# Program order of an expert chain: the usual side last, a hint for its first branch, narrower turns

## The chip, the cores and the metric

The kernel runs on one core of one Trainium2 chip. The metric is the device time of one execution in microseconds (us); less is better. Engines are called as the profile calls them: PE (TensorE), DVE (VectorE), ACT (ScalarE), POOL (GpSimd), SP (SyncE, which issues most transfers). Each engine has a sequencer that reads its own stream of instructions, and that stream is fetched from memory while the program runs. The trace shows what a sequencer itself does (branches, register loads, semaphores) under PEldq, DVEq, ACTq, POOLq and SPq.

## What is computed

Three layers follow each other, all in float32:

```
x   = attention(q, k, v)             # chunks of 64 tokens, 8 heads, 2 x 576 = 1152 tokens of 512
x   = moe(x, w_gate, w1, w2, cap)    # 8 experts, top 1, at most 288 tokens each
out = sum over e of p[:, e] * (relu(x @ w1[e]) @ w2[e])      # 4 domain experts, dense
```

In the middle layer the expert of a token is the argmax of its gate logits, the tokens of an expert are taken in order until its capacity of 288 is full, the others give zero rows, and a kept row is `gate * (relu(x @ w1[e]) @ w2[e])` with w1 of 512 x 1024 and w2 of 1024 x 512. How many tokens an expert gets is known only on the chip.

## The kernel before, in words

**Products.** Every float32 factor is split into a high part (rounded, dtype fp32r, by ScalarE, `part_hi`, line 114) and a low rest (by VectorE, `part_lo`, line 118), and a product is the sum of high x high, high x low and low x high.

**Attention** (lines 325 to 391) goes over nine blocks of 128 tokens. It also makes the gate logits, the rank of every token in its expert, and one-hot sums `t_ps` that give the tokens of each expert. Expert 0 of the program's order is the one that token 0 chose (`oh0`), so its weights are loaded early. Lines 394 to 445 then count: `cnt` is the tokens of an expert (`n_ps`, cut at the capacity), `large` says whether `cnt` is over `limit` (232 for the first expert, 192 for the others), `form` is 0 for an expert without tokens, 1 for a small and 2 for a large one, and the others are put in the order large, small, empty. PE meanwhile runs 27 products on zeros (`warm`, line 140). `form`, the sum of all tokens (`kept`) and the places of the experts' columns (`o_r`) become registers in lines 768 to 770 (`numbers`, line 545): each engine loads them itself.

**The experts** (lines 520 to 784). `wide(k, W, slots)` computes one expert on W columns with three products per weight tile; `joined(k, W, slots)` does it for at most 192 tokens with two, of 384 and 192 columns, since the high and the low part of x stand side by side. After each eighth or fourth of the work both call `place(i)`, which issues what `chores` (line 667) has put into slot i: the weights of the next expert (load, high, low), and the turn of the next expert's tokens. A turn (`xturn`, line 536) transposes the gathered rows in three pieces of 128, 128 and 32 tokens, for four column blocks; `xsplit` (line 541) makes high and low out of 288 columns. `gather` (line 400) fetches the rows by three indirect transfers.

**The order of the code around the change.** The program holds every sequence of forms as nested branches. `expert_0` stands twice (lines 780 to 783): in the first place for a first expert of at most 232 tokens (chain "a"), in the second for a larger one (chain "b"). Each calls `large_from(1, left, tag)`, which nests "large_k" branches while experts can still be large (`left`, here 5 and 4), and at every depth an Else with `small_from`, which nests "more_k" branches of joined experts. Where no expert with tokens is left, `first_dense` (line 716) computes the first dense layer-1 products, 48 of 384 columns, on the banks. All these ends go through a jump to the code behind the chain, then through line 780's to `late` (line 653: the high and low parts of the second dense weights) and `pick_last` (line 925), which chooses the dense program by `kept`. A branch is written so that its "then" side follows in memory and its Else is jumped to. `hint` (line 664) puts an instruction on PE, early in an expert, that tells its sequencer by a register which side of the next branch is to come: 1 the following code, 0 the Else.

**The dense layers** (line 796 on) are 4 domains x 2 halves x 3 groups of up to 384 tokens: layer 1 is line 824, layer 2 lines 853 and 872. Their first bank is one that first_dense used, so the first product waits until VectorE's line 726 has read it.

With the inputs timed here the first expert has 210 tokens, one other is large (384, cut to 288), four are small and two are empty. So the path is: chain "a", `wide(0, 232)`, "large_1" taken, `wide(1, 288)`, the Else of "large_2", four `joined`, the Else of "more_6", `first_dense`, and out.

Of the kernel before, what the change touches and what calls it, by code (L numbers as in the profile page):

```python
# [9 lines left out]
F32 = mybir.dt.float32  # L10
F32R = mybir.dt.float32r
F16 = mybir.dt.float16
I32 = mybir.dt.int32
ACTF = mybir.ActivationFunctionType
ALU = mybir.AluOpType
AX = mybir.AxisListType
PSUM = bass.MemoryType.PSUM
DRAM = bass.MemoryType.DRAM
ENG = mybir.EngineType

P = 128
NTOK = 1152
# [5 lines left out]
KD = DM // P  # L28
NE = 8
# [7 lines left out]
EPS = 1e-9  # L37
MC = 6
NP = NE + 1
WARM = (8, 4, 2, 27, 4, 3, 4)  # L40

C_ID = 0
C_IO = 128
# [27 lines left out]
def kernel(ctx: ExitStack, tc: tile.TileContext, kqv_d, wg, w_all, dp, cst, out, cap):  # L71
    nc = tc.nc

    XW, W0, CW = 288, 232, 192
    wins = ((0, P), (P, P), (2 * P, XW - 2 * P))
    assert cap <= XW

    ctx.enter_context(tc.manual_schedule(engines={ENG.PE, ENG.Activation, ENG.DVE, ENG.SP}))
# [4 lines left out]
    cp = ctx.enter_context(tc.tile_pool(name="cp", bufs=1))  # L83
    wp = ctx.enter_context(tc.tile_pool(name="wp", bufs=1))
    xrp = ctx.enter_context(tc.tile_pool(name="xrp", bufs=1))
    sp = ctx.enter_context(tc.tile_pool(name="small", bufs=3))

    xt0 = xrp.tile([P, 2 * KD * XW], F32R, name="xt0")
    xrs = [xrp.tile([P, 3, DM], F32, name=f"xr{j}") for j in range(2)]
    cc = cp.tile([P, C_KEEP], F32, name="cc")  # L90
    ident = cc[:, C_ID:C_ID + P]
# [8 lines left out]
    oh0 = cp.tile([P, NE], F32, name="oh0")  # L100
# [4 lines left out]
    wz = cp.tile([P, 512], F16, name="wz")  # L105
# [14 lines left out]
    def bc(ap, n, pos):  # L120
        return ap.unsqueeze(pos).broadcast_to(list(ap.shape[:pos]) + [n] + list(ap.shape[pos:]))


    with ExitStack() as ast:
        ap_ = ast.enter_context(tc.tile_pool(name="attn", bufs=2))
# [10 lines left out]
        def warm(n, tag="s"):  # L136
            if n:
                w_ps = ps.tile([P, 512], F32, tag=tag, bufs=2 if tag == "s" else 1, name="w_ps")
                for i in range(n):
                    nc.tensor.matmul(w_ps, wz[:, 0:P], wz, start=True, stop=True)  # L140
# [184 lines left out]
        for j in range(NT):  # L325
            if 1 <= j < 3:
                warm(WARM[1], "xt")
            a, b, c, d = j, j - 1, j - 2, j - 3
# [41 lines left out]
        n = NT - 1  # L370
# [26 lines left out]
        with nc.allow_low_precision(reason="whole numbers below 2048"):  # L397
            nc.vector.tensor_reduce(out=gidx0, in_=g0, axis=AX.X, op=ALU.add)

        def gather(k, ws=(0, 1, 2)):  # L400
            for w in ws:
                n = wins[w][1]
                ix = gidx[0:n, k, w:w + 1] if k else gidx0[0:n, w:w + 1]
                nc.gpsimd.indirect_dma_start(out=xrs[k % 2][0:n, w, :], out_offset=None, in_=x_d[:, :],  # L404
                                             in_offset=bass.IndirectOffsetOnAxis(ap=ix, axis=0))
# [10 lines left out]
        some, cnt, place, off, form = (st[:, i] for i in range(5))  # L416
        rol2 = sp.tile([P, NE], F32, bufs=1, name="rol2")
        large = sp.tile([P, NE], F32, bufs=1, name="large")
        pr = sp.tile([P, 2, NE, NE], F32, bufs=1, name="pr")
        sel = sp.tile([P, NE, NE], F32, bufs=1, name="sel")  # L420
        pv = sp.tile([P, 3, NE, NE], F32, bufs=1, name="pv")
# [4 lines left out]
        nc.vector.tensor_scalar(out=some, in0=n_ps[:, 0], scalar1=0.0, scalar2=None, op0=ALU.is_gt)  # L426

        nc.vector.tensor_tensor(out=large, in0=cnt, in1=limit, op=ALU.is_gt)
        nc.vector.scalar_tensor_tensor(out=rol2, in0=large, scalar=-8.0, in1=rol, op0=ALU.mult, op1=ALU.add)
        nc.vector.tensor_tensor(out=mrol, in0=bc(rol2, NE, 1), in1=bc(rol2, NE, 2), op=ALU.is_lt)  # L430
        nc.vector.tensor_tensor(out=pr, in0=bc(mrol, 2, 1), in1=bc(st[:, 0:2], NE, 2), op=ALU.mult)
# [88 lines left out]
    with ExitStack() as est:  # L520
# [12 lines left out]
            nc.scalar.copy(hi, src)  # L533
            nc.vector.tensor_tensor(out=lo, in0=src, in1=hi.bitcast(F32), op=ALU.subtract)

        def xturn(k, kd, t, ws):
            for w in ws:
                lo, n = wins[w]
                nc.tensor.transpose(t[:, lo:lo + n], xrs[k % 2][0:n, w, kd * P:kd * P + P], ident[0:n, 0:n])  # L539

        def xsplit(k, kd, t, a=0, b=XW):
            hi_lo(xts[k % 2][:, kd, 0, a:b], xts[k % 2][:, kd, 1, a:b], t[:, a:b])

        def numbers(src, **kw):
            return nc.values_load_multi_w_load_instructions(
                src, min_val=0, skip_runtime_bounds_check_because="whole numbers counted on the chip, within it for any routing", **kw)[1]

        regs = []

# [114 lines left out]
        def hint(label, off):  # L664
            tc.mark_branch_hint_location(label, hint=off, engines=(ENG.PE,))

        def chores(k, small, ahead):

            slots = {}

            def at(i, f, *args):
                slots.setdefault(i, []).append(lambda: f(*args))

            def turn(kd):
                xturn(k + 1, kd, tps[kd % 2], range(3))

            def split(kd):
                xsplit(k + 1, kd, tps[kd % 2])

            def known():  # L680
                regs[:] = numbers(pli[0:1, :], engines=(ENG.SP,), max_val=NE + NDOM - 1)

            if k + 1 < NE:
                for kd in range(KD):
                    at((7, 9, 11, 13)[kd], turn, kd)
                    at((8, 10, 12, 14)[kd], split, kd)
            if k == 0:
                at(0, part_lo, 2, 0)
                at(0, places)
                at(0, known)  # L690
                for h in range(2):
                    at(0, load, 1, 0, h)
                at(1, part_lo, 2, 1)
                for h in range(2):
                    at(1, load, 1, 2, h)
                for n, (j, h) in enumerate(((1, 0), (1, 1), (3, 0), (3, 1))):
                    at(n + 3, part_lo, j, h)
                    at(n + 3, load, 1, j, h)
            else:
                for n, (j, h) in enumerate(((1, 0), (1, 1), (3, 0), (3, 1))):  # L700
                    at((0, 2, 5, 7)[n], part_hi, j, h)
                    i = (1, 3, 6, 8)[n]
                    at(i, part_lo, j, h)
                    at(i, load, k + 1, j, h)
            for n, (j, h) in enumerate(((0, 0), (0, 1), (2, 0), (2, 1))):
                at((8, 9, 11, 13)[n], part_hi, j, h)
                i = (9, 10, 12, 14)[n]
                at(i, part_lo, j, h)
                at(i, load, k + 2, j, h)
            at(3, ahead)  # L710
            if k == 0:
                for n, f in enumerate(dense_rows()):
                    at(7 + n // 2, f)
            return slots

        def first_dense():

            for ff in range(NF):
                o = banks[ff][:, 0:GW]
                c = 0  # L720
                for kd in range(KD):
                    for a, b in ((0, 0), (0, 1), (1, 0)):
                        nc.tensor.matmul(o, w1(0, a, kd)[:, ff * P:ff * P + P], x2[:, b, kd, 0:GW], start=c == 0, stop=c == 3 * KD - 1)  # L723
                        c += 1
                nc.scalar.activation(out=h_first[:, ff, 0], in_=o, func=ACTF.Relu)
                nc.vector.scalar_tensor_tensor(out=h_first[:, ff, 1], in0=o, scalar=0.0, in1=h_first[:, ff, 0].bitcast(F32),
                                               op0=ALU.max, op1=ALU.subtract)

        def ahead(k):
            if 1 < k + 1 < NE:  # L730
                gather(k + 1)

        def small_from(k, tag):
            if k == NE:
                first_dense()
                return
            with tc.If(form_r[k] > 0, label=f"more{tag}_{k}") as more:
                ahead(k + 1)
                joined(k, CW, chores(k, True, lambda: hint(f"more{tag}_{k + 1}", form_r[k] + form_r[k + 1] - 1) if k + 1 < NE else None))
                small_from(k + 1, tag)  # L740
            with more.Else():
                first_dense()

        def large_from(k, left, tag):
            if k == NE or not left:
                small_from(k, f"{tag}_{k}")
                return
            with tc.If(form_r[k] > 1, label=f"large{tag}_{k}") as large:
                ahead(k + 1)
                wide(k, XW, chores(k, False, lambda: hint(f"large{tag}_{k + 1}", form_r[k + 1] // 2) if k + 1 < NE and left > 1 else None))  # L750
                large_from(k + 1, left - 1, tag)
            with large.Else():
                small_from(k, f"{tag}_{k}")

        def expert_0(W, left, tag):

            wide(0, W, chores(0, False, lambda: hint(f"large{tag}_1", form_r[1] // 2)))
            scatter(meta_d, [(posi[:, i:i + 1], meta[:, i]) for i in range(NT)], [])
            nc.gpsimd.dma_start(out=mcol, in_=meta_d.rearrange("(i p) c -> p i c", p=P))
            large_from(1, left, tag)  # L760
# [8 lines left out]
        kept = numbers(ovi[0:1, 0:1], max_val=NTOK)  # L769
        o_r = numbers(ovi[0:1, 1:1 + NE], engines=(ENG.Activation, ENG.DVE), max_val=NTOK)  # L770
        ts = (*banks[4:6], *tps)
        for w in range(3):
            for kd in range(KD):
                xturn(0, kd, ts[kd], (w,))
            for i in range((WARM[6], 0, 0)[w]):
                nc.tensor.matmul(banks[2], wz[:, 0:P], wz, start=True, stop=True)
        for kd in range(KD):
            xsplit(0, kd, ts[kd])
        gather(2)
        with tc.If(form_r[0] < 2, label="first") as first:  # L780
            expert_0(W0, (NTOK - 1) // (CW + 1), "a")
        with first.Else():
            expert_0(XW, (NTOK - W0 - 1) // (CW + 1), "b")
        late(NE)


# [191 lines left out]
```

## Time and profile before

| | |
|---|---|
| median of 3 runs | 592.49 us (591.46 to 592.79) |
| the profiled execution | 588.06 us, span 586.3 us |
| mean granted PE clock | 0.994 |
| PE busy | 565.5 us (96%), 3651 products |
| DVE / ACT / POOL busy | 310.4 / 197.6 / 68.2 us |
| instruction fetches | 38 packets of 16 KB on queue q8, 43 of 8 KB on q14 |

The stages by the timeline: attention and counting to 59.5 us, first expert from 62.2, second from 84.0, four joined experts from 114.7, first_dense from 198.6, dense layers from 214.2. In the chain of waits, "issue" is time in which the engine waited for nothing that the profile shows; the fetch of code is such a time. A branch row of a sequencer (COMPARE_BRANCH, jumps too) has its duration in nanoseconds as minimum/median/maximum. For PE this duration holds the wait for the code behind the branch; for DVE and ACT it doesn't, and the wait is seen from the start of what comes next. A PE sequencer runs a few us ahead of PE itself.

### The profile page before, as it was taken

How to read it: one execution, taken by the hardware profiler on the slowest of the kernel's cores; microseconds unless marked ns; L12 is line 12 of the kernel's file. 1: busy time of each engine (PE TensorE's matmuls, PEld its weight loads, DVE VectorE, ACT ScalarE, POOL GpSimd, SP SyncE). 2: the span in 40 equal slices, each digit the busy share in tenths (PEclk: the TensorE clock that was granted, in tenths of full speed). 3: DMA queues.
4: the chain of work that ended last, by engine and by line, in shares of the span. 5: the costliest groups of instructions: out<-in, count | busy, mean ns of one | idle time of the engine just before them, and what ended most of it. 6: DMA issues, size and time to landing. Idle time of an engine off the chain costs nothing.

```text
span 586.3 us, 9383 instructions
## 1 busy us (share of the span) xinstructions
PE 565.5 (96%) x3651; PEld 516.9 (88%) x3651; DVE 310.4 (53%) x654; ACT 197.6 (34%) x429; POOL 68.2 (12%) x63
## 2 busy tenths in 40 slices
PE   7999999999999869999999999999999999999994
PEld 4786899999999768898899899899899889889983
DVE  5898775578888524433524534533533543454221
ACT  5785245387778431112112112112111211211110
POOL 3322807201213000000000000000000000000032
PEclk9999999999999989999999999999999999999998
DMA  8881495757767506002202101211210000000022
GB/s 331 311 287 59 140 355 117 260 164 270 244 214 231 194 16 212 1 1 72 73 1 72 59 14 37 72 36 37 73 36 1 1 1 1 1 0 1 1 91 76
DMA packets 17361, 61.02 MB, mean 104 GB/s; under 512 B 2864, under 2 KB 3008, under 8 KB 16640
## 3 DMA queue, kind: packets, MB, share of 16 engines
q1 hardware_dynamic: 14688, 52.91, 26.4%
q0 software_dynamic: 2592, 7.14, 3.9%
q8 instruction: 38, 0.62, 0.5%
q14 instruction: 43, 0.35, 0.2%
HBM read 55.29 MB, written 4.75 MB: 102 GB/s over the span
## 4 chain that ended last, share of the span: by engine, by line
PE 91%; DVE 3%; issue 2%; DMA 1%; POOL 0%; ACT 0%; SPq 0%; POOLq 0%; DVEq 0%; ACTq 0%
PE pg L824 30%; PE po L853 22%; PE bank L608 9%; PE po L872 9%; PE bank L570 8%; PE bank L609 4%; PE tp L539 2%; PE bank L723 1%; PE w_ps L140 1%; PE s_ps L209 1%; DMA kqv<-in_kqv 1%; PE o_ps L231 1%; PE lr_ps L259 1%; PE et_ps L223 1%; PE xt_ps L252 1%
## 5 line engine op out<-in xcount | busy, mean ns | idle before, releaser
L824 PE MATMUL pg<-x,hl 128*128 128x384 f32 (+1 forms) x1104 | 181.2, 324 | 5.2 <-issue 5.2
L824 PEld LDWEIGHTS pg<-x,hl 128*128 128x128 f32 x1104 | 178.2, 189 | 6.7 <-issue 5.4
L118 DVE TENSOR_TENSOR hl<-raw,hl 128x1024 fp32r<-128x1024 f32 x80 | 96.7, 1218 | 12.5 <-ACT hl L114 12.4
L114 ACT CAST hl<-raw 128x1024 fp32r<-128x1024 f32 x80 | 81.9, 1049 | 6.7 <-issue 6.7
L853 PE MATMUL po<-hl,htb 128*128 128x512 f32 x288 | 68.7, 396 | 0.0
L853 PE MATMUL po<-hl,h_other 128*128 128x512 f32 (+1 forms) x300 | 68.5, 386 | 0.0
L853 PEld LDWEIGHTS po<-hl,h_other 128*128 128x128 f32 x300 | 54.6, 188 | 12.1
L853 PEld LDWEIGHTS po<-hl,htb 128*128 128x128 f32 x288 | 53.9, 188 | 12.4
L860 DVE SCALAR_TENSOR_TENSOR xr<-po,mcol,xr 128x512 f32<-128x512 f32 (+1 forms) x43 | 31.7, 738 | 58.9 <-PE po L853 58.2
L834 ACT ACTIVATE h_other<-pg 128x384 fp32r<-128x384 f32 x32 | 15.6, 491 | 90.8 <-PE pg L824 90.8
L834 ACT ACTIVATE htb<-pg 128x384 fp32r<-128x384 f32 x28 | 13.8, 492 | 86.4 <-PE pg L824 86.4
L835 DVE SCALAR_TENSOR_TENSOR h_other<-pg,h_other 128x384 fp32r<-128x384 f32 x32 | 17.6, 557 | 44.2 <-ACT h_other L834 44.2
L608 PE MATMUL bank<-htb,hl 128*128 128x384 f32 x128 | 39.1, 370 | 0.0
L835 DVE SCALAR_TENSOR_TENSOR htb<-pg,htb 128x384 fp32r<-128x384 f32 x28 | 15.6, 558 | 42.9 <-ACT htb L834 42.9
L608 PE MATMUL bank<-xt,hl 128*128 128x384 f32 x128 | 37.1, 362 | 0.0
L404 POOL DMA_INDIRECT xr<-x_d,gidx x24 | 26.8, 1118 | 84.9 <-PE tp L539 60.2
L881 POOL MEMSET raw<- 128x512 f32 x1 | 0.5, 524 | 287.5 <-DVE hl L118 287.5
L609 PE MATMUL bank<-htb,hl 128*128 128x192 f32 x128 | 32.1, 251 | 0.0
L609 PE MATMUL bank<-xt,hl 128*128 128x192 f32 x128 | 32.0, 250 | 0.0
L878 DVE TENSOR_TENSOR rest<-po,rest 128x288 f32<-128x288 f32 x28 | 12.8, 457 | 26.4 <-PE po L872 26.4
L872 PE MATMUL po<-h_other,hl 128*128 128x288 f32 x192 | 26.0, 295 | 0.0
L872 PE MATMUL po<-htb,hl 128*128 128x288 f32 x192 | 26.0, 295 | 0.0
(171 smaller groups left out, 699.9 us busy)
## 6 DMA issues: line engine op xcount, KB each, us to landing
raw<-in_w_all SPq DMA_DIRECT2D x72, 512.0 KB, 3.8
kqv<-in_kqv SPq DMA_DIRECT2D x8, 768.0 KB, 8.3
raw<-in_w_all SPq DMA_DIRECT2D x4, 1024.0 KB, 5.0
x_d<-x SPq DMA_DIRECT2D x9, 256.0 KB, 2.0
xt<-meta_d SPq DMA_DIRECT2D x1, 1056.0 KB
kqv<-in_kqv SPq DMA_DIRECT2D x3, 256.0 KB
xr<-x_d,gidx POOLq DMA_INDIRECT x24
ca<-in_cst SPq DMA_DIRECT2D x1, 320.0 KB
```

The costliest lines, as they stand in the source:

```text
L114: nc.scalar.copy(hls[j][:, 0, a:b], raws[j][:, a:b])
L118: nc.vector.tensor_tensor(out=hls[j][:, 1, a:b], in0=raws[j][:, a:b], in1=hls[j][:, 0, a:b].bitcast(F32), op=ALU.subtract)
L404: nc.gpsimd.indirect_dma_start(out=xrs[k % 2][0:n, w, :], out_offset=None, in_=x_d[:, :], in_offset=bass.IndirectOffsetOnAxis(ap=ix, axis=0))
L570: nc.tensor.matmul(o, wt(a), t[:, b, 0:W], start=start and i == 0, stop=stop and i == len(PAIRS) - 1, skip_group_check=True)
L608: nc.tensor.matmul(o, wt(0), t[:, :, 0:W], start=start, stop=False, skip_group_check=True)
L609: nc.tensor.matmul(o[:, 0], wt(1), t[:, 0, 0:W], start=False, stop=stop, skip_group_check=True)
L824: nc.tensor.matmul(pg[:, 0:n], w1(u % 2, a, kd)[:, ff * P:ff * P + P], x2[:, b, kd, g * GW:g * GW + n], start=c == 0, stop=c == 3 * KD - 1)
L834: nc.scalar.activation(out=h[:, ff, 0], in_=pg[:, 0:GW], func=ACTF.Relu)
L835: nc.vector.scalar_tensor_tensor(out=h[:, ff, 1], in0=pg[:, 0:GW], scalar=0.0, in1=h[:, ff, 0].bitcast(F32), op0=ALU.max, op1=ALU.subtract)
L853: nc.tensor.matmul(po, h[:, ff, a, tt * P:tt * P + P], w2(u % 2, b, ff)[:, cols], start=c == 0, stop=c == 3 * NF - 1)
L860: nc.vector.scalar_tensor_tensor(out=acc[t][:, cols], in0=po, scalar=pe, in1=acc[t][:, cols], op0=ALU.mult, op1=ALU.add)
L872: nc.tensor.matmul(po[:, 0:W], w2(u % 2, b, ff)[:, d * P:d * P + P], h[:, ff, a, 0:W], start=c == 0, stop=c == 3 * NF - 1)
```

## The change

1. The two copies of `expert_0` change places: "first" now asks for the large first expert, whose chain "b" follows in memory, and the usual chain "a" is its Else, the last code ahead of `late`.
2. The rare chains are short. `left` is 1 for "a": after two large experts every further one with tokens is computed wide. For "b" (-1) all are wide from the start. `small_from` stands at two depths of "a" only.
3. The first expert's flag (`lf`, `f0i`) is counted on its own by two VectorE operations, PE loads it and gets a hint for "first"; the 27 warm products are cut into 16 ahead of the load and 11 behind the hint.
4. A joined expert turns, splits and gathers 192 columns of the next expert (pieces of 128 and 64) where it did 288.
5. `xturn` takes a width in place of a list of pieces; the first expert's turns keep their order. `numbers` is moved up.

```diff
-WARM = (8, 4, 2, 27, 4, 3, 4)
+WARM = (8, 4, 2, 16, 4, 3, 4, 11)
...
-        def gather(k, ws=(0, 1, 2)):
-            for w in ws:
-                n = wins[w][1]
+        def gather(k, W=XW):
+            for w, lo in enumerate(range(0, W, P)):
+                n = min(P, W - lo)
...
         nc.vector.tensor_tensor(out=large, in0=cnt, in1=limit, op=ALU.is_gt)
+        nc.vector.tensor_tensor(out=lf, in0=large, in1=oh0, op=ALU.mult)
+        with nc.allow_low_precision(reason="whole numbers below 2048"):
+            nc.vector.tensor_reduce(out=f0i, in_=lf, axis=AX.X, op=ALU.add)
+        f0_r = numbers(f0i[0:1, 0:1], engines=(ENG.PE,), max_val=1)
+        tc.mark_branch_hint_location("first", hint=f0_r[0], engines=(ENG.PE,))
+        warm(WARM[7])
...
-        def xturn(k, kd, t, ws):
-            for w in ws:
-                lo, n = wins[w]
-                nc.tensor.transpose(t[:, lo:lo + n], xrs[k % 2][0:n, w, kd * P:kd * P + P], ident[0:n, 0:n])
+        def xturn(k, kd, t, W, first=0):
+            for lo in range(first, W, P):
+                n = min(P, W - lo)
+                nc.tensor.transpose(t[:, lo:lo + n], xrs[k % 2][0:n, lo // P, kd * P:kd * P + P], ident[0:n, 0:n])
...
-        def chores(k, small, ahead):
+        def chores(k, small, ahead, W=XW):
...
-                xturn(k + 1, kd, tps[kd % 2], range(3))
+                xturn(k + 1, kd, tps[kd % 2], W)
...
-                xsplit(k + 1, kd, tps[kd % 2])
+                xsplit(k + 1, kd, tps[kd % 2], 0, W)
...
             with tc.If(form_r[k] > 0, label=f"more{tag}_{k}") as more:
-                ahead(k + 1)
-                joined(k, CW, chores(k, True, lambda: hint(f"more{tag}_{k + 1}", form_r[k] + form_r[k + 1] - 1) if k + 1 < NE else None))
+                ahead(k + 1, CW)
+                joined(k, CW, chores(k, True, lambda: hint(f"more{tag}_{k + 1}", form_r[k] + form_r[k + 1] - 1) if k + 1 < NE else None, CW))
...
+        def look(k, left, tag):
+            if k < NE:
+                hint(f"large{tag}_{k}", (form_r[k] + int(left < 0)) // 2)
+
         def large_from(k, left, tag):
-            if k == NE or not left:
-                small_from(k, f"{tag}_{k}")
+            if k == NE:
+                first_dense()
                 return
-            with tc.If(form_r[k] > 1, label=f"large{tag}_{k}") as large:
+            with tc.If(form_r[k] > int(left >= 0), label=f"large{tag}_{k}") as large:
                 ahead(k + 1)
-                wide(k, XW, chores(k, False, lambda: hint(f"large{tag}_{k + 1}", form_r[k + 1] // 2) if k + 1 < NE and left > 1 else None))
+                wide(k, XW, chores(k, False, lambda: look(k + 1, left - 1, tag)))
                 large_from(k + 1, left - 1, tag)
             with large.Else():
-                small_from(k, f"{tag}_{k}")
+                if left >= 0:
+                    small_from(k, f"{tag}_{k}")
+                else:
+                    first_dense()
...
-        with tc.If(form_r[0] < 2, label="first") as first:
-            expert_0(W0, (NTOK - 1) // (CW + 1), "a")
+        with tc.If(form_r[0] > 1, label="first") as first:
+            expert_0(XW, -1, "b")
         with first.Else():
-            expert_0(XW, (NTOK - W0 - 1) // (CW + 1), "b")
+            expert_0(W0, 1, "a")
         late(NE)
```

## Rows read from the trace of the kernel before

**Rows 1.** The page, part 4: the chain that ended last, by engine.
```profile
PE 91%; DVE 3%; issue 2%; DMA 1%; POOL 0%; ACT 0%; SPq 0%; POOLq 0%; DVEq 0%; ACTq 0%
```
**Rows 2.** The chain that ended last, 196 to 216 us: start, us, what.
```profile
198.57 1.63 PE bank L723 x8
200.19 1.73 issue
201.92 7.11 PE bank L723 x40
...
209.57 0.57 DVE htb L726
210.14 4.03 issue
```
**Rows 3.** The chain, whole run: two dense layer-1 stretches of 48 products of 384.
```profile
214.17 9.86 PE pg L824 x48
...
247.26 8.32 PE pg L824 x48
```
**Rows 4.** Branches of PE's sequencer between 194 and 214 us (ns, starts), by line.
```profile
L737 PEldq COMPARE_BRANCH  x1: 3489/3489/3489, 194.9 to 194.9; - x1
...
L737 PEldq COMPARE_BRANCH  x1: 3338/3338/3338, 205.8 to 205.8; - x1
...
L780 PEldq COMPARE_BRANCH  x1: 4654/4654/4654, 209.2 to 209.2; - x1
```
**Rows 5.** Stretches at the dense layers' start; last three numbers: PEclk, DMA share, GB/s.
```profile
209.00:213.50 4.50, 0.01 (x1) 0.00 (x0) 0.56 (x1) 0.49 (x1) 0.00 (x0) 1.00 0.07 13
213.50:217.00 3.50, 2.83 (x9) 2.86 (x10) 0.00 (x0) 0.79 (x1) 0.00 (x0) 0.51 0.07 16
```
**Rows 6.** Waits of PE, whole run: line and tile, waited for, us, times, longest.
```profile
PE bank L723 <- ACT x L533: 1.1, 1, 1.1
```
**Rows 7.** One turn of a joined expert on PE (timeline), and the first of sixteen in the chain.
```profile
194.40 0.27 PE L539 MATMUL tp<-cc,xr 128*128 128x128 f32 x1
...
194.51 0.45 PE L539 MATMUL tp<-cc,xr 128*128 128x128 f32 x2
...
123.99 0.40 PE tp L539 x3
```
**Rows 8.** A taken jump, the branch large_2: PE's and VectorE's sequencers, and VectorE's next branch.
```profile
L748 PEldq COMPARE_BRANCH  x1: 404/404/404, 112.3 to 112.3; - x1
...
L748 DVEq COMPARE_BRANCH  x1: 67/67/67, 115.4 to 115.4; - x1
...
L737 DVEq COMPARE_BRANCH  x1: 50/50/50, 118.6 to 118.6; - x1
```
**Rows 9.** The branch named "first" on the sequencers of PE and VectorE.
```profile
L780 PEldq COMPARE_BRANCH  x1: 95/95/95, 60.9 to 60.9; - x1
...
L780 DVEq COMPARE_BRANCH  x1: 60/60/60, 63.1 to 63.1; - x1
```
**Rows 10.** Timeline of VectorE at the start of the first expert.
```profile
64.65 0.40 DVE L583 SCALAR_TENSOR_TENSOR htb<-bank,htb 128x232 fp32r<-128x232 f32 x1 [0.91 <-ACT htb L582]
...
67.61 1.22 DVE L118 TENSOR_TENSOR hl<-raw,hl 128x1024 fp32r<-128x1024 f32 x1
```
**Rows 11.** The chain at the start of the first expert.
```profile
61.87 0.34 issue
...
68.88 4.95 PE bank L570 x42
```
**Rows 12.** Line 570 on PE: what it waited for besides issue (us, times).
```profile
  DVE hl L118: 0.2, 1
```
**Rows 13.** Before the branch: warm products, PE's register loads, one small VectorE operation.
```profile
53.51 5.99 PE L140 MATMUL w_ps<-wz 128*128 128x512 f16 x27
...
L545 PEldq TENSOR_LOAD <-ovi x2: 318/1232/2146, 56.7 to 59.0; - x2
...
54.16 0.17 DVE L428 TENSOR_TENSOR large<-st,limit 128x8 f32<-128x8 f32 x1
```

More of the change, by code (lines that the diff above doesn't have):

```diff
@@ L74 @@
     XW, W0, CW = 288, 232, 192
-    wins = ((0, P), (P, P), (2 * P, XW - 2 * P))
     assert cap <= XW
@@ L121, in bc, with numbers @@
         return ap.unsqueeze(pos).broadcast_to(list(ap.shape[:pos]) + [n] + list(ap.shape[pos:]))
+    def numbers(src, **kw):
+        return nc.values_load_multi_w_load_instructions(
+            src, min_val=0, skip_runtime_bounds_check_because="whole numbers counted on the chip, within it for any routing", **kw)[1]
     with ExitStack() as ast:
@@ L418 @@
         large = sp.tile([P, NE], F32, bufs=1, name="large")
+        lf = sp.tile([P, NE], F32, bufs=1, name="lf")
+        f0i = cp.tile([P, 1], I32, name="f0i")
         pr = sp.tile([P, 2, NE, NE], F32, bufs=1, name="pr")
@@ L534, in hi_lo @@
             nc.vector.tensor_tensor(out=lo, in0=src, in1=hi.bitcast(F32), op=ALU.subtract)
-        def xturn(k, kd, t, ws):
-            for w in ws:
-                lo, n = wins[w]
-                nc.tensor.transpose(t[:, lo:lo + n], xrs[k % 2][0:n, w, kd * P:kd * P + P], ident[0:n, 0:n])
+        def xturn(k, kd, t, W, first=0):
+            for lo in range(first, W, P):
+                n = min(P, W - lo)
+                nc.tensor.transpose(t[:, lo:lo + n], xrs[k % 2][0:n, lo // P, kd * P:kd * P + P], ident[0:n, 0:n])
         def xsplit(k, kd, t, a=0, b=XW):
             hi_lo(xts[k % 2][:, kd, 0, a:b], xts[k % 2][:, kd, 1, a:b], t[:, a:b])
-        def numbers(src, **kw):
-            return nc.values_load_multi_w_load_instructions(
-                src, min_val=0, skip_runtime_bounds_check_because="whole numbers counted on the chip, within it for any routing", **kw)[1]
         regs = []
@@ L727, in first_dense, with ahead @@
                                                op0=ALU.max, op1=ALU.subtract)
-        def ahead(k):
+        def ahead(k, W=XW):
             if 1 < k + 1 < NE:
-                gather(k + 1)
+                gather(k + 1, W)
         def small_from(k, tag):
@@ L742, in small_from @@
                 first_dense()
+        def look(k, left, tag):
+            if k < NE:
+                hint(f"large{tag}_{k}", (form_r[k] + int(left < 0)) // 2)
         def large_from(k, left, tag):
-            if k == NE or not left:
-                small_from(k, f"{tag}_{k}")
+            if k == NE:
+                first_dense()
                 return
-            with tc.If(form_r[k] > 1, label=f"large{tag}_{k}") as large:
+            with tc.If(form_r[k] > int(left >= 0), label=f"large{tag}_{k}") as large:
                 ahead(k + 1)
-                wide(k, XW, chores(k, False, lambda: hint(f"large{tag}_{k + 1}", form_r[k + 1] // 2) if k + 1 < NE and left > 1 else None))
+                wide(k, XW, chores(k, False, lambda: look(k + 1, left - 1, tag)))
                 large_from(k + 1, left - 1, tag)
             with large.Else():
-                small_from(k, f"{tag}_{k}")
+                if left >= 0:
+                    small_from(k, f"{tag}_{k}")
+                else:
+                    first_dense()
         def expert_0(W, left, tag):
-            wide(0, W, chores(0, False, lambda: hint(f"large{tag}_1", form_r[1] // 2)))
+            wide(0, W, chores(0, False, lambda: look(1, left, tag)))
             scatter(meta_d, [(posi[:, i:i + 1], meta[:, i]) for i in range(NT)], [])
@@ L771 @@
         ts = (*banks[4:6], *tps)
-        for w in range(3):
+        for kd in range(KD):
+            xturn(0, kd, ts[kd], P)
+        for i in range(WARM[6]):
+            nc.tensor.matmul(banks[2], wz[:, 0:P], wz, start=True, stop=True)
+        for lo in (P, 2 * P):
             for kd in range(KD):
-                xturn(0, kd, ts[kd], (w,))
-            for i in range((WARM[6], 0, 0)[w]):
-                nc.tensor.matmul(banks[2], wz[:, 0:P], wz, start=True, stop=True)
+                xturn(0, kd, ts[kd], min(lo + P, XW), lo)
         for kd in range(KD):
```

## The prediction

> **What bounds the kernel now.** I read the chain of waits by engine first: PE holds 91% of it [rows 1]. An edit therefore pays only if it removes PE work, removes a stretch in which PE stands still, or keeps its clock up. So the second view is the chain where the experts end and the dense layers begin, and there PE stands still. The last joined expert is followed by eight products of first_dense, a stall of 1.73 us, the other forty products until 201.92 + 7.11 = 209.03, and then nothing until 214.17: 5.1 us, of which 4.03 come after VectorE has freed the last bank at 209.57 + 0.57 = 210.14 [rows 2, 3]. The third view, PE's sequencer alone, tells what it did meanwhile. Three branches held it: the one to first_dense 3.49 us, the jump out of the nested branches 3.34, the jump of line 780 over the other half of the program (the large first expert) 4.65 [rows 4]. The sequencer runs ahead of PE, so the first of these is partly covered; the next two follow each other with nothing queued. [...]
>
> The inputs take the small-first-expert side: the trace holds products of 232 columns, one more wide expert, then four joined ones. That side was the fall-through of "first"; after the change it is the taken jump, and it lies last.
>
> **The change, part by part**, against the profiled execution (588.06 us, span 586.3).
>
> **1. Leaving the experts.** The line-780 jump goes: the usual chain now runs into the code behind it. One jump out of the nested branches stays. With first_dense issued as before, it starts at 205.8 and ends about 209.1 [rows 4]. The next product must also wait for the bank freed at 210.14 [rows 2], which is later. So the dense layers start about 0.1 us after that, at 210.25 instead of 214.17: 3.9 us gained. The idle falls from 5.1 to 1.2 us; a stall of 1.73 left the clock at 1.00 [rows 2, 5], so I take the 9.86 - 8.32 = 1.5 us back too. Gain 5.4; bounds 0 (the stay at 4.65 comes back under another jump) and 5.4. ScalarE's and VectorE's one jump instead of two stays beside PE's first 8 us of products.
>
> **2. Entering first_dense.** The code lies elsewhere, so the 1.73 us stall (code that was not there after sixteen instructions) and the 3.49 us at the branch may go or move. Ahead of the first of the eight products PE waits 1.1 us, which the profile puts down to ScalarE's x2 columns [rows 6]; the branch's 3.49 us end in the same stretch, so a part of the 1.1 may be code and a part is data. Without either, at best 1.1 + 1.7 = 2.8 us are saved; at worst the stall in mid-code becomes a whole jump's, 3.3 instead of 1.7, a loss of 1.6. I take 1.5 gained, nearly the stall in mid-code alone: that it should fall so soon behind the landing again has no reason in the diff, while the data wait stays.
>
> **3. The joined experts.** In four of them, four turns each, 3 transposes become 2, of 128 and 64 columns. Two full ones start 194.51 - 194.40 = 0.11 us apart; the whole turn takes 0.40 in the chain [rows 7]. 16 x 0.11 = 1.8 us gained, on the path because PE is; bounds 1.0 and 2.7 (0.06 and 0.17 each, a third of the turn being 0.13). The narrower splits and two gathers instead of three run on ScalarE, VectorE and POOL, which wait for PE there: nothing. If that cover were gone, the last split would cost about 0.1 us.
>
> **4. Entering the first expert.** Here the change charges. PE gets a hint. Of the two taken and hinted branches the trace has, one took 0.40 us [rows 8], the other 3.49 [rows 4]; I go with the first, because the hint comes some 4 us (flag about 54.7, its load 2.15 [rows 13]) ahead of a branch at 60.9 [rows 9], and a fetch cost 3.3. The others get no hint. VectorE took the jump at large_2 at 115.4 and reached its next branch at 118.6 [rows 8]: 3.2 us. Its "first" branch is at 63.1 [rows 9], so it resumes at about 66.4 instead of 64.65 [rows 10]: 1.75 us late. Queued behind it are the ReLU remainder, the low half of the third weight part, eight small operations, and the second piece of that low half, which ends at 67.61 + 1.22 = 68.83 [rows 10]. PE takes up at 68.88, having waited 0.2 us for just that operation [rows 11, 12]. So the delay goes through: PE stalls until about 70.5, and 1.6 to 1.8 is lost; I take 1.8. ScalarE is late by about 0.8 us, with six banks to spare. SP's weight loads start 1.75 later and are wanted as much later; POOL's jump stands beside its memset.
>
> [...]
>
> **5. Flag, load, hint.** Two more small VectorE operations (0.17 us for a like one [rows 13]) put off every engine's register loads by up to 0.4 us. PE's own load of the flag (one like it took 2.15 us [rows 13]) is covered by 16 warm products of 5.99 / 27 = 0.22 us, 3.5 us together; uncovered it would cost up to 2.2. The first transposes wait for the gather, not the loads. I take 0.2; bounds 0 and 0.6.
>
> **Sum.** -5.4 - 1.5 - 1.8 + 1.8 + 0.2 = -6.7 us. The profiled execution would take 581.4. The median of the runs shown is 592.49, 4.4 above it, a distance the change doesn't touch: 592.49 - 6.7 = 585.8. What a measurement of this kernel can tell from no change is about 0.2%, 1.2 us.
>
> **The rivals.**
> **The hint comes to nothing.** PE stalls at "first" as at the jumps: 60.9 + 3.4 and 0.3 to the first product make 64.6 where it began after the 0.34 us [rows 11], at 62.2. That is 2.4 lost; VectorE's delay then hides inside it. 2.4 instead of 1.8: 586.4, or 587.9 if that idle also halves the clock. For it: the 3.49 us branch was hinted. Chance 0.25.
> **The first jump is free.** If VectorE's fetch is done while its splits run, part 4 costs nothing: 584.0. Against it: 3.2 us at the other jump [rows 8]. Chance 0.12.
> **The last jump keeps its price.** The change then fails at its main end: two waits for code still stand between first_dense and the dense layers, and part 1 is 0: 592.49 - 1.3 = 591.2. For it: PE has stalled right after a landing once (1.73 us [rows 2]). Chance 0.1.
> **Slower: a landing pays twice.** The 1.73 us stall shows that code behind a landing can be missing as well. If that befalls VectorE's landing in the first expert (3.3 more, so PE idles 5 us there and loses the 1.5 of the halved clock) and PE's last landing (part 1 is 0), the sum is -1.5 - 1.8 + 1.8 + 3.3 + 1.5 + 0.2 = +3.5: 596.0. It decides once both landings fall shortly ahead of code not yet fetched; one alone leaves the kernel faster. Chance 0.06.
> The forecast has the remaining 0.47.
>
> **How the numbers follow.** The forecast's own bounds: part 2 from -2.8 to +1.6, part 3 from -2.7 to -1.0, part 5 from 0 to 0.6, not all at one end, give 584.0 to 589.2. The range reaches to the free first jump with 1.2 of the 1.3 that part 2 can still bring (582.8) and to the last jump's rival (591.2): 582.8 to 591.3. Faster by over 0.2% (below 591.3): forecast 0.47, hint 0.25, free jump 0.12, and 0.02 of the last jump's rival: 0.86, and I give 0.84 for what I have not thought of. Same: most of that rival, 0.08. Slower: 0.08.
>
> **What would show it.** Right: between first_dense and the first dense product PE idles about 1.2 us, with one long branch of its sequencer, the granted clock stays at 1.00 and that stretch takes 8.3 us; each joined turn takes about 0.29 in the chain; in the first expert PE waits about 1.8 us for the low-half subtraction (line 118 of before), and VectorE's first ReLU remainder starts near 66.4. Wrong: two branches over 3 us still in a row at the end; a PE start of the first expert at 64 or later; a clock of half speed in either place; a stall in mid-code where there was none.

## The result, and the profile after

The changed kernel takes 584.91 us (median of 5 runs, 581.18 to 585.28), the kernel before on the same chip 591.60 (5 runs); the ratio is 0.987, interval 0.983 to 0.990. The prediction was 585.8, from 582.8 to 591.3. Its sign and size came out, but not by its own sum: the way out of the experts came close, the way into first_dense gave more than forecast and the turns less, and the first expert cost 3.0 us where 1.8 were forecast.

The profiled execution of after took 585.28 us. Its span is 583.5 where that of before is 586.3, only 2.8 less. The trace of after has 3.9 us more in the attention stage, whose code is the same: there the granted clock (third number from the end) was at half for 6.8 us, and in before it was not. Before, then after:

```profile
9.80:16.60 6.80, 6.60 (x73) 4.50 (x73) 5.03 (x12) 4.97 (x16) 4.48 (x3) 1.00 1.03 405
```

```profile
9.80:16.60 6.80, 5.97 (x39) 4.33 (x40) 3.27 (x8) 3.19 (x11) 3.06 (x2) 0.50 1.04 416
```

From PE's first turn of tokens (its first transpose of gathered rows, at 59.55 us before and 63.48 after) to the end it is 520.04 us against 526.73: 6.69 less. So everything below is measured from that first turn, by the starts of the stages' first products on the timeline:

| us | before | after | difference |
|---|---|---|---|
| first turn to second expert | 27.20 | 30.16 | +2.96 |
| second expert | 27.93 | 27.95 | 0.0 |
| joined experts, to the first product of first_dense | 83.89 | 81.36 | -2.53 |
| first_dense | 10.45 | 9.45 | -1.00 |
| PE idle behind it | 5.16 | 1.26 | -3.90 |
| first 48 dense products and the 36 of layer 2 behind them | 18.10 | 16.83 | -1.27 |
| the rest of the dense layers | 354.0 | 353.0 | -1.0 |

The last row has no edit in it. Over all the traces of this study it lies between 352.4 and 354.0, so its 1.0 belongs to the execution, not to the change.

**The end of the experts.** The chain of after, 204 to 222 us (start, us, what):

```profile
204.70 0.28 DVE x L545
205.02 7.40 PE bank L730 x41
212.44 0.50 ACT htb L732
212.96 0.57 DVE htb L733
213.53 0.14 issue
213.67 8.58 PE pg L840 x48
```

Against [rows 2]: the stall in the middle of first_dense is gone, and so are the 4.03 us of "issue" behind the freed bank; 0.14 is left. The dense products now start as soon as VectorE's read of line 733 has let the bank go, and 48 of them take 8.58 us where they took 9.86 [rows 3]. PE's waits name that read as what ended the idle time; a shorter wait for data is left inside first_dense (line and tile, waited for, us, times, longest):

```profile
PE pg L840 <- DVE htb L733: 1.3, 1, 1.3
...
PE bank L730 <- DVE x L545: 0.7, 1, 0.7
PE bank L577 <- DVE hl L117: 0.2, 1, 0.2
```

PE's sequencer has two branches there, where [rows 4] had three (ns minimum/median/maximum):

```profile
L744 PEldq COMPARE_BRANCH  x2: 880/2300/3720, 200.6 to 209.1; - x2
```

The long one, 3.72 us from 209.1, ends at 212.9, ahead of the bank's release at 213.53. The granted clock stays up, where [rows 5] showed 0.51 (columns as there):

```profile
209.00:213.50 4.50, 3.40 (x20) 3.08 (x18) 1.45 (x3) 0.98 (x2) 0.00 (x0) 1.00 0.03 9
213.50:217.00 3.50, 3.33 (x19) 3.36 (x20) 0.77 (x2) 1.82 (x2) 0.00 (x0) 1.00 0.04 12
```

**The first expert.** The branch "first" on three sequencers, which [rows 9] showed at 95 and 60 ns:

```profile
L796 PEldq COMPARE_BRANCH  x1: 2117/2117/2117, 65.4 to 65.4; - x1
L796 ACTq COMPARE_BRANCH  x1: 55/55/55, 65.9 to 65.9; - x1
L796 DVEq COMPARE_BRANCH  x1: 72/72/72, 67.1 to 67.1; - x1
```

The chain there:

```profile
67.72 3.64 issue
71.35 0.05 DVEq L590
...
71.55 0.40 DVE htb L590
...
74.59 1.14 DVE hl L117
75.73 0.04 issue
75.78 4.96 PE bank L577 x42
```

Call the time from a taken branch to the engine's next instruction its landing. VectorE branched at 67.09 and its next instruction behind the jump is at 71.35: 4.26 us for the landing. ScalarE's ReLU (70.57 + 0.36) had been there 0.6 before VectorE's remainder at 71.55, so VectorE's own landing set that start. From there the queue is that of [rows 10], up to the second low-half piece, and PE takes up 0.04 us behind it. Yet PE itself hardly waited, 0.2 us (the third wait above), because it was late too:

```profile
67.70 7.89 PE L577 MATMUL bank<-xt,hl 128*128 128x232 f32 x54 [1.86 <-DVE xt L545]
```

The profile names VectorE's last split, which ended at about that time; but the first product needs only the first pieces, and those came as early behind the turn as before. What came last is the sequencer, held by the branch until 65.4 + 2.1 = 67.5. Then the clock fell to half:

```profile
67.80:71.20 3.40, 3.40 (x17) 3.40 (x18) 0.00 (x0) 0.36 (x1) 3.40 (x1) 0.50 0.15 41
71.20:75.50 4.30, 4.30 (x39) 4.21 (x38) 3.85 (x12) 1.09 (x3) 3.92 (x2) 1.00 0.02 6
```

So two delays of about 3 us each end side by side near 75.6: PE's (its first product 4.22 us behind the turn, 2.66 before: 1.56, and 1.7 by the clock) and VectorE's (first remainder 8.07 us behind the turn, 5.10 before: 2.97). From one trace it can't be told which of them to cure.

### The profile page after: what moved, and what is told of

It is laid out like the page before. It is cut to its first block, busy times and chain, and to the rows that moved or that the text cites. A ratio compares the mean times of both kernels' runs of the same rounds, so it can differ in the third digit from the quotient of the medians.

```text
span 583.5 us, 9341 instructions
## 1 busy us (share of the span) xinstructions
PE 566.9 (97%) x3635; PEld 517.5 (89%) x3635; DVE 309.0 (53%) x656; ACT 196.8 (34%) x429; POOL 65.1 (11%) x59
## 4 chain that ended last, share of the span: by engine, by line
PE 84%; issue 2%; DVE 2%; POOL 0%; ACTq 0%; ACT 0%; POOLq 0%; DVEq 0%
PE pg L840 30%; PE po L869 22%; PE bank L615 9%; PE po L888 9%; PE bank L577 7%; PE bank L616 4%; PE tp L550 1%; PE bank L730 1%; DVE hl L117 1%; POOL out L510 0%; ACTq L124 0%; DVE xt L545 0%; PE po L903 0%; POOLq L990 0%; DVE xr L876 0%
## 5 line engine op out<-in xcount | busy, mean ns | idle before, releaser
L407 POOL DMA_INDIRECT xr<-x_d,gidx x20 | 23.1, 1156 | 85.9 <-PE tp L550 62.2
L577 PE MATMUL bank<-xt,hl 128*128 128x232 f32 (+1 forms) x192 | 25.8, 298 | 2.0 <-DVE xt L545 1.9
L577 PEld LDWEIGHTS bank<-xt,hl 128*128 128x128 f32 x192 | 25.3, 201 | 2.3 <-issue 1.9
```

The costliest lines, as they stand in the source:

```text
L577: nc.tensor.matmul(o, wt(a), t[:, b, 0:W], start=start and i == 0, stop=stop and i == len(PAIRS) - 1, skip_group_check=True)
```

## The experiments

Eleven runs were made in three groups, each group on a chip with its own runs of before; two of them repeat the changed kernel and one repeats another. "Start" below is the start of the second expert after the first turn, 27.20 before and 30.16 after. Where no landing is in it, it is 27.19 or 27.20 in four traces. The times of a kernel scatter between runs, by 1.1 us (nohint) to 6.5 us (turn288), so what is worth 1 to 3 us is read from the traces, by stage.

**Narrower turns alone undone.**

```diff
-                ahead(k + 1, CW)
-                joined(k, CW, chores(k, True, ..., CW))
+                ahead(k + 1)
+                joined(k, CW, chores(k, True, ...))
```

> The changed kernel, but a joined expert turns, splits and gathers 288 columns again. If the narrower turns are worth PE's time (forecast), the four joined experts take 1.4 to 1.8 us more than the 81.4 us from their first product to first_dense, each turn 0.40 in the chain instead of 0.31, and the whole about 1.5 us more. If the turns hide beside other work, nothing changes.

Measured: 586.24 us, ratio to before 0.989 (0.983 to 0.995). The joined stretch takes 82.76 us, 1.40 more than after's 81.36, and a turn in the chain is 0.39 again. Line of it, then of after:

```profile
200.68 0.39 PE tp L550 x3
```

```profile
200.33 0.31 PE tp L550 x2
```

So 16 turns give 1.4 us, 0.09 each. Not intended: PE stood 3.72 us at "first" here, though this edit doesn't touch it, and start is 32.34.

**Flag, load and hint away.** The 27 warm products stand in one piece, `lf`, `f0i`, `f0_r` and the hint are gone.

> The changed kernel without the flag, its load and the hint on PE (27 warm products in one piece). If the hint fetched a part of the landing, PE's sequencer stands about 3.4 us at the branch named first instead of 2.1, its first product comes 1.3 us later, and since PE waited only 0.2 us for VectorE, the first expert ends about 1.1 later. If VectorE's own landing sets the end, 0 to 0.3 later. If the hint does nothing, 2.1 us at the branch as before and the same time.

Measured: 584.40 us, 0.989 (0.985 to 0.993). PE stands 3.95 us at "first", the clock halves for 3.4 us, start is 31.26:

```profile
L788 PEldq COMPARE_BRANCH  x1: 3952/3952/3952, 62.7 to 62.7; - x1
```

Against this the hint as the change gives it is worth 1.1 us in the trace of after, but nothing that the times can tell, and nothing in turn288, whose start is later than this one.

**The two chains in the old order**, without flag and hint, all else as changed:

```diff
-        with tc.If(form_r[0] > 1, label="first") as first:
-            expert_0(XW, -1, "b")
-        with first.Else():
+        with tc.If(form_r[0] < 2, label="first") as first:
             expert_0(W0, 1, "a")
+        with first.Else():
+            expert_0(XW, -1, "b")
```

> The changed kernel (short rare chains, 192-column turns), but the usual chain again in the first place and fallen through to, without flag and hint. If the order made the gain, the entry into the first expert gets its 3.0 us back and the way to the dense layers its two waits for code and the halved clock (5.2 us): 2.2 us slower than the changed kernel. If shorter code made it, the way out stays at 1.3 us and it is 3.0 us faster.

Measured: 587.51 us, 0.991 (0.988 to 0.994). Start is 27.20, exactly as before. At the end both long branches are there again, and the wait for code, and the halved clock (branches of PE by line, the chain, the windows):

```profile
L736 PEldq COMPARE_BRANCH  x2: 441/1976/3510, 196.2 to 204.7; - x2
```

```profile
L788 PEldq COMPARE_BRANCH  x1: 4901/4901/4901, 208.3 to 208.3; - x1
```

```profile
208.55 0.57 DVE htb L725
209.12 4.46 issue
213.57 10.55 PE pg L832 x45
```

```profile
212.20:219.00 6.80, 5.42 (x17) 5.46 (x18) 1.29 (x2) 2.37 (x3) 0.00 (x0) 0.50 0.05 11
```

PE idles 5.59 us. The plainest comparison is with nohint, which ran on the same chip and differs in the order of the two chains alone: 587.51 us against 584.40, and from the first turn to the end 524.45 against 521.11. Against the trace of after the old order is 4.4 us slower where 2.2 were expected: the idle and the slowed products cost 6.8 where 5.2 were counted, and 0.6 us more is a stall inside a joined expert. So with short chains in both, the order makes the gain at the end and the loss at the start; that the chains became shorter makes neither. The new order with the long chains was not run. first_dense takes 9.46 us here as in after and follows the last joined expert at once: that its stall is missing comes with the rest of the change, not with the order.

**A hint for VectorE and ScalarE beside the change.** Both load a zero in the fifth attention block and are told by it that the Else is to come; in the trace the hint runs right behind that load, at 29.5 us on ScalarE and 33.0 on VectorE:

```diff
+            if j == 4:
+                z_r = numbers(wz[0:1, 0:2].bitcast(I32), engines=(ENG.DVE, ENG.Activation), max_val=1)
...
+        tc.mark_branch_hint_location("first", hint=z_r[0], engines=(ENG.DVE, ENG.Activation))
```

> The changed kernel with a hint for the Else of the branch named first also on VectorE and ScalarE, from a register loaded in the middle of the attention. If such a hint is kept, VectorE's first operation behind the branch comes 3 to 4 us earlier than its 8.1 us after the first turn, and PE no longer waits for VectorE; but PE's own start, 4.2 us after the first turn at half clock, then sets the end, so only about 0.2 us is gained. If hints only act shortly ahead, VectorE stands at the branch as long as without.

Measured: 584.94 us, 0.988 (0.983 to 0.993). VectorE's landing is cured: 0.64 us from its branch to what follows. ScalarE's is not (3.8). But PE, with the same instructions as in after, now stands 3.65 us, not 2.12, and the clock is at half for 6.8 us:

```profile
L799 PEldq COMPARE_BRANCH  x1: 3648/3648/3648, 65.0 to 65.0; - x1
L799 ACTq COMPARE_BRANCH  x1: 73/73/73, 65.5 to 65.5; - x1
L799 DVEq COMPARE_BRANCH  x1: 84/84/84, 66.7 to 66.7; - x1
```

```profile
67.20:74.00 6.80, 5.08 (x24) 5.11 (x25) 1.83 (x5) 0.36 (x1) 6.64 (x2) 0.50 0.09 29
```

Start is 32.14, with no wait of PE for the low half left; the first ReLU waits for PE there (ScalarE landed 2.6 us ahead of it). PE's landing alone cost 32.14 - 27.20 = 4.9 us here, more than the 2.96 of after.

**The changed kernel again**, for the spread of that stay.

> The changed kernel once more, beside its variants on one chip. Its profile showed PE's sequencer 2.1 us at the branch named first, two variants with the same hint 3.7. If the hint from the flag fetches ahead, 2.1 us come again; if it does nothing there, 3.3 to 4.0 us, as without it.

Measured: 583.20 us, 0.988 (0.982 to 0.994). 1.92 us at the branch, clock half for 3.4, start 30.23. A late hint has thus left about 2 us twice here and 3.7 in the two kernels above. The trace names no engine for a packet of code; the one of queue q8 that lies at the branch is taken as PE's. By that the fetch of PE's code begins 0.3 to 0.5 us ahead of the branch in the first kind (65.08 for 65.4 in after) and 1.2 to 1.3 behind it in the second. Without any hint it begins 1.3 behind it too, so in turn288 and veht the hint came to nothing.

The hint was not too late by the prediction's measure. Its instruction in after:

```profile
L990 PEldq BRANCH_PREFETCH_HINT  x1: 49/49/49, 59.3 to 59.3; - x1
```

That is 6.1 us ahead of the branch at 65.4, and 6.1 to 6.5 in all five traces with this hint, since PE's load of the flag took 0.48 us and not the 2.15 that the prediction took for it; and without a hint PE stood 3.95 us. So the hint did not start its fetch at once. What decides whether it starts ahead of the branch stays open.

**PE's hint alone, given early** from a register that holds zero, in the eighth of the nine attention blocks (pe7, `j == 7`) or in the fifth (pe4, `j == 4`), without the flag:

```diff
+            if j == 7:
+                z_r = numbers(wz[0:1, 0:2].bitcast(I32), engines=(ENG.PE,), max_val=1)
+                tc.mark_branch_hint_location("first", hint=z_r[0], engines=(ENG.PE,))
```

> The changed kernel without the flag; PE's hint for the Else of the branch named first comes from a register loaded at the end of the eighth attention block, so earlier in the code by more than the stretch in which the flag's hint lay. If a hint only acts when the sequencer goes over into the next piece of code, it now acts: PE stands under 0.5 us at the branch, its first product comes about 2.7 us after the first turn, with no halved clock, and only VectorE's late landing is left: the second expert begins about 28.9 to 29.9 us after the first turn (changed kernel 30.2, before 27.2). If a hint ahead of this branch does nothing at all, 3.3 to 4.0 us at the branch and 31 to 32.

> As the run before, but the register is loaded and the hint given three attention blocks earlier, several pieces of code ahead. If a hint waits for the piece that holds its branch, the same as there; if it acts at the next piece whatever that is, it is spent by then and PE stands 3.3 to 4.0 us.

Measured: 583.20 (0.986, 0.981 to 0.991) and 584.18 (0.989, 0.983 to 0.994). PE stands 0.39 us at "first" in both. The hint runs 21 us ahead of the branch in pe7 and 34 in pe4. In pe7 it is the first of these two (the other belongs to a later branch):

```profile
L985 PEldq BRANCH_PREFETCH_HINT  x2: 37/41/45, 42.2 to 68.8; - x2
```

In every trace of the changed order one packet of queue q8 begins 11 to 13 us ahead of the branch (52.9 in after, for 65.4); these hints run before it, the late ones after it (59.3 in after). Distance alone does not decide: the hint for the jump to first_dense ran 16 us ahead of its branch in the kernel before, where PE stood 3.49 us [rows 4], and in swap, where it stood 0.44.

At the first product behind the jump PE now waits for VectorE, as the prediction had it. The wait and its chain in pe7, then those of pe4:

```profile
PE bank L572 <- DVE hl L117: 1.6, 1, 1.6
```

```profile
73.09 4.95 PE bank L572 x42
```

```profile
PE bank L572 <- DVE hl L117: 1.7, 1, 1.7
```

```profile
71.59 6.58 PE bank L572 x42
```

Start is 28.75 in pe7, 1.55 more than before. In pe4 it is 30.72, because the same wait was followed by a halved clock, and 42 products took 6.58 us in place of 4.95:

```profile
72.40:75.90 3.50, 3.50 (x20) 3.50 (x19) 2.76 (x5) 0.73 (x2) 2.48 (x2) 0.51 0.91 283
```

**All three engines hinted early**: PE at `j == 7`, VectorE at `j == 4`, ScalarE ahead of the attention loop.

> The changed kernel without the flag, with early hints on PE (end of the eighth block), VectorE (fifth) and ScalarE (ahead of the first). If the landings of PE and VectorE make the whole loss at the first expert, the second expert begins 27.2 to 27.6 us after the first turn as in the kernel before, 2.6 to 3.0 us earlier than in the changed kernel, and the whole takes that much less. If something else of the move is behind it (the register loads, the place of the code), 29 to 30 stay.

Measured: 580.82 us (4 runs), 0.983 (0.978 to 0.987), the changed kernel of that group 583.20. PE stands 0.39 us, what waited is gone, start is 27.19:

```profile
L796 PEldq COMPARE_BRANCH  x1: 394/394/394, 63.5 to 63.5; - x1
L796 ACTq COMPARE_BRANCH  x1: 73/73/73, 64.2 to 64.2; - x1
L796 DVEq COMPARE_BRANCH  x1: 84/84/84, 65.5 to 65.5; - x1
```

```profile
65.04 6.16 PE bank L577 x52
71.20 0.02 issue
71.21 4.95 PE bank L577 x42
```

This is [rows 11] again, with the usual chain still behind the taken jump.

**That kernel and the changed one in more rounds, and the same without ScalarE's hint.**

> The changed kernel again, beside the one with all three hints given early. Both theories: about 583 to 585 us, some 7.5 below the kernel before. PE's stay at the branch first will again be either about 2 us (fetch under way before the branch) or about 3.7 (fetch begun behind it); in both cases the second expert begins 30 to 32.4 us after the first turn of tokens, against 27.2 before.

> The early hints for PE, VectorE and ScalarE once more, in more rounds. If the 2.96 us that the first jump cost are what separates it from the changed kernel: second expert 27.2 us after the first turn, time about 3 us (0.5%) below the changed kernel of the same chip. If the earlier difference (580.82 against 583.2) was the noise of single runs: equal within 1 us.

> PE and VectorE get their early hints, ScalarE gets none. If ScalarE's landing is hidden behind its free banks, as the prediction had it: second expert 27.2 us after the first turn, the time of the kernel with all three hints. If it binds (VectorE's first ReLU remainder waits for ScalarE's, which then starts about 6.2 us after the turn instead of 2.4, so the low half of the weights behind it in VectorE's queue is late again): second expert at 29 to 29.5, and about 2 us lost against all three hints.

Measured: changed 584.36 us (6 runs, 0.987, 0.984 to 0.990), all three hints 582.68 (5 runs, 0.984, 0.981 to 0.988), without ScalarE's 583.36 (5 runs, 0.985, 0.982 to 0.988). Starts: 29.76, 27.19 and 28.92. Early hints give back the whole price of the first landing in both their traces; in time it is 2.4 and 1.7 us of the medians, with intervals that overlap, so the times alone do not show it. Without ScalarE's hint the median is 0.7 longer than with all three, where 2 were expected: the trace shows that loss, the times do not. The joined experts of the two traces with all three hints are 0.3 to 0.5 us longer than after's, which was not followed up.

Without its hint ScalarE's landing binds. Its first ReLUs, two at once, and VectorE's remainder behind them:

```profile
69.02 0.62 ACT L587 ACTIVATE htb<-bank 128x232 fp32r<-128x232 f32 x2 [2.91 <-PE bank L575]
```

```profile
69.42 0.40 DVE L588 SCALAR_TENSOR_TENSOR htb<-bank,htb 128x232 fp32r<-128x232 f32 x1 [2.63 <-ACT htb L587]
```

ScalarE branched at 65.0 and VectorE's own code was there 0.6 us after its branch at 66.2; the 2.6 us that VectorE idles are ScalarE's. (The profile puts ScalarE's idle time down to a bank of PE that was done long before.)

## Why the prediction was right, and where it was wrong

**Part 1, leaving the experts: right, shown.** Forecast 5.4; measured 3.90 of idle and 1.27 of clock, 5.2 together. Idle of 1.26 us, one long branch, the clock at 1.00 and VectorE's read as the new limit are what the prediction named; only the stretch takes 8.58 where 8.3 was named. The old order brings everything back. The rival by which the last jump keeps its price is out. The one taken jump that is left held PE's sequencer 3.72 us, the last one of the old order 4.90 in swap. Of the forecast 5.4, 3.9 was idle and 1.5 what the slower stretch of [rows 3] takes longer, its start at a clock of 0.51 [rows 5].

**Part 2, entering first_dense: right in kind, too small.** Forecast 1.5. The stretch from the last joined product to the end of first_dense lost a gap of 1.15 us and 1.00 of its length, together 2.15. The stall in mid-code went, as assumed; the term that was mis-sized is the data wait, of which 1.1 was to stay [rows 6]: 0.7 stayed, and inside the products rather than ahead of them.

**Part 3, the turns: right in kind, too large.** 1.4 for 1.8. The forecast took a whole piece of 0.11 off each turn; a turn of 128 and 64 columns is only 0.09 shorter than one of 128, 128 and 32.

**Part 4, the first expert: the step that failed is "PE gets a hint", priced like the cheaper of two hinted branches ("I go with the first").** PE stood 2.12 us in after, 1.9 in two more traces and 3.65 and 3.72 in another two, never 0.40, and its clock halved in all five. The reason given, that the hint comes some 4 us ahead and a fetch costs 3.3 [rows 4], fails as well: it came 6.1 us ahead and the fetch still began only 0.3 us before the branch. With PE's stay cured by an early hint, the rest of the step stands in pe7: VectorE's landing, the queue behind it and a wait of 1.6 us, at a cost of 1.55 where 1.8 was forecast. The second mis-sized term is the landing itself: VectorE's took 4.26 us in after, 2.9 to 4.4 over the traces, where [rows 8] gave 3.2. Third, "ScalarE is late by about 0.8 us, with six banks to spare" is wrong: the spare banks did not help, because VectorE's queue waits for ScalarE's first ReLU, 2.63 us in pv, and pv, where that ReLU starts 1.7 us later than before, loses 1.73 by that alone. It cost nothing in pe7, where VectorE landed later still (its remainder starts 0.7 us after that ReLU's end). In sum the landing cost 2.96 with the flag, for 2.0; so the rival of a free first jump is out.

The rival by which the hint comes to nothing was priced at 2.4, or 3.9 with the clock; without the hint it is 31.26 - 27.20 = 4.06. So that price was good. In after the truth lay between forecast and rival; in turn288 and veht the rival came in full, with a loss of 5.1 and 4.9, and the clock at half for 6.8 us, twice as long as without the hint. A hint given early enough did bring the code in time: 0.39 to 0.40 us at the branch in four kernels, 3.95 without any.

**Part 5, the flag: forecast 0.2, measured 0.0.** From `n_ps` to the first turn it is 6.08 us, 6.07 before.

**The sum.** -5.2 - 2.1 - 1.4 + 3.0 = -5.7; the 1.0 of the dense layers that no edit explains makes the -6.7 between these two traces. Between the medians it is 6.7 as well, by the ratio 6.0 to 9.9. The forecast's -6.7 thus agrees with the times, but by its terms it was 1 us too good, and that last 1 us is not traced to any step. That forecast and medians meet at 6.7 is in part luck: the terms' misses offset each other in part, and runs that scatter by over 1 us can't tell 5.7 from 6.7.

## What to carry to other kernels

In this kernel the usual path belongs last in the nest of branches, so that it runs out into what follows: what the second jump out cost at the end, where nothing else is queued, is idle time and clock (3.90 and 1.27 us). The price is one taken jump at the start, and it has to be looked up for every engine that takes it, not for PE alone: whichever landed last set the time, and curing one only showed the next (start 28.75 with PE's cured, 28.92 with PE's and VectorE's, 27.19 with all three). A hint 6 us ahead of its branch was too late here (PE stood 1.9 to 3.7 us) and one 20 us or more ahead was in time on PE for this branch (0.39), though how far is far enough was not found. Where the likely side is known a hint needs no data at all, only a register with a constant, as in pe7 and early, and each engine wants its own (without one ScalarE landed 3.8 us behind its branch in pv). What a constant hint costs when the other side comes was not run, nor any input with a large first expert.

## What was not expected of the hardware

- The jump of "first" cost VectorE 2.9 to 4.4 us, ScalarE 2.9 to 3.9 and PE 3.65 to 3.95 where its fetch was not ahead of it. With a hint in the attention stage or ahead of it this fell to 0.64, 0.47 and 0.39.
- A hint can come to nothing: ScalarE's in the fifth attention block did (3.8 us), the one ahead of the attention loop worked (0.47). Why was not settled.
- Waits of PE of 1.6 to 1.9 us at the first expert were followed by a halved clock in some traces (after: 1.86 us, 3.4 us at 0.50; pe4: 1.7 and 0.51) and not in others (pe7 1.6, pv 1.7), at 1.6 to 1.7 us of cost. The halved stretches lasted about 3.4 or 6.8 us. The prediction had counted 1.73 us as safe.
